# Three loads per group of an attention kernel moved to the ends of transposes through Pool's instruction order, and the load of K two units later

## The chip, the cores and the metric

One NeuronCore of a Trainium2 chip. The metric is the device time of one execution in microseconds (us), as the median of several executions. Engines: PE multiplies matrices, ACT computes exponentials, DVE does elementwise vector work, Pool (GpSimd) here only small statistics and the issue of loads, SP only the issue of transfers.

## The reference, cut to what matters

```python
h = _layernorm(x) * (1 + ca) + sa            # x: 2048 x 512, bf16
q = (h @ wq) in 32 heads of 128              # 8 groups: 4 q heads share one K and one V
p = softmax(q k^T * 128**-0.5)               # 2048 x 2048 for each head
x = x + ga * ((p v) @ wo)
...                                          # then a gMLP block: w_in, gelu, w_sp, w_out
```

A group needs its K (2048 x 128), V (the same), a slice of wq (512 x 512) and one of wo (512 x 512), 512 KB each in bf16.

## The kernel before

It runs 128 attention units: unit u is group u // 16 and query tile u % 16 (128 queries, 4 heads). A unit has 8 slots; in each slot PE does a piece of the scores of unit u, of the product with V of an earlier unit, and of the q or output projection. Even units from 8 on are "row units": their scores come with queries in rows, DVE scales the rows, and a DMA transpose on SP's queue (a **turn**) writes them as PE needs them. Such a unit has four turns, one for each head, and PE multiplies by V three units later.

```python
TURN_A, TURN_B = 2 * CT, NU - 2                      # 8 and 126
def by_rows(u):  return TURN_A <= u < TURN_B and u % 2 == 0
def pv_at(u):    return u + 3 if by_rows(u) else u + 1
def wo_at(u):    return pv_at(u) + (3 if u < TURN_B - CT else 2)
...
# in qk(u, i), for a row unit, after the second half of head hh (slots i = 1, 3, 5, 7):
if half == 1:
    at(*divmod(u * NSLOT + i + 2, NSLOT), lambda: turn_rows(u, hh))
...
def turn_rows(u, hh):
    ...                                              # row sum, reciprocal
    nc.vector.tensor_scalar(out=rows, in0=rows, scalar1=rinv, scalar2=None, op0=ALU.mult)
    nc.sync.dma_start_transpose(out=pTs[u][:, :, hh * P : (hh + 1) * P], in_=rows)
...
def load_v(g):                                       # two buffers; wq_g and wo_g likewise
    v1 = late.tile([P, NKT, DV], BF16, name="v1")
    nc.gpsimd.memset(v1[:, :, DH:DV], 1.0)
    ...                                              # group 0 has two transfers on SP
    nc.gpsimd.dma_start(out=v1[:, :, 0:DH], in_=v_dram[:, g])
    ...
def load_k(g):
    kT = early.tile([P, SK], BF16, name="kT")
    nc.sync.dma_start_transpose(out=kT[:], in_=A_k_cache[0, g])
...
for g in range(1, HKV):
    it = (g - 1) * NT                                # first unit of the group before
    at(it + 9, 5, lambda g=g: load_k(g))
    at(*((5, 2) if g == 1 else (it + 7, 4)), lambda g=g: load_wq(g, nc.gpsimd))
    at(*((5, 2) if g == 1 else (it + 11, 4)), lambda g=g: load_v(g))
    at(*((5, 2) if g == 1 else (it + 13, 4)), lambda g=g: load_wo(g, nc.gpsimd))
```

`at(unit, slot, fn)` sets a place in the program's order. It is not a time: an engine runs ahead of the others until a semaphore stops it.

## Time and profile before

| | before |
|---|---|
| time, median | 1314.8 us (3 runs, 1313.14 to 1316.12) |
| span of the profiled execution | 1312.3 us |
| PE, ACT, DVE, Pool busy | 1294.0, 1113.0, 689.3, 55.7 us |
| all waits of PE that the trace lists | some 4 us |
| landing of a turn, median and longest | 4.5 and 12.1 us |
| least slack of a turn, units 20 to 116 | 2.3 us (unit 68) |

**Slack** is the time from the landing of a unit's last turn to the start of the first matmul that reads it. It comes from adding a transpose's issue time and its issue-to-landing time, and comparing with PE's start.

The busy time by stretch shows the stage that matters (us of the stretch, its length, busy time and instructions of PE, weight loads, DVE, ACT and Pool, granted clock, share of the DMA engines, GB/s):

```profile
100.00:1100.00 1000.00, 992.74 (x7224) 567.70 (x7359) 508.05 (x1267) 975.88 (x1385) 25.54 (x37) 1.00 0.79 143
```

PE is full, ACT is nearly so (975.88 of 1000), and the DMA engines are used to 79%. The table of transfers (what, issuer, count, size, median us to landing) has the loads that the change moves:

```profile
wq_g<-in_A_wq_dram POOLq DMA_DIRECT2D x7, 512.0 KB, 6.2
v<-in_A_v_cache_dram POOLq DMA_DIRECT2D x7, 512.0 KB, 6.9
wo_g<-in_A_wo_dram POOLq DMA_DIRECT2D x7, 512.0 KB, 8.4
```

The same 512 KB take longest as wo. In group 5 wo is issued in the middle of a unit's turns, wq beside the last turn of one (both at 528.9 us), and V just after the turns of one have landed.

### The profile page before, as it was taken

How to read it: one execution, taken by the hardware profiler on the slowest of the kernel's cores; microseconds unless marked ns; L12 is line 12 of the kernel's file. 1: busy time of each engine (PE TensorE's matmuls, PEld its weight loads, DVE VectorE, ACT ScalarE, POOL GpSimd, SP SyncE). 2: the span in 40 equal slices, each digit the busy share in tenths (PEclk: the TensorE clock that was granted, in tenths of full speed). 3: DMA queues.
4: the chain of work that ended last, by engine and by line, in shares of the span. 5: the costliest groups of instructions: out<-in, count | busy, mean ns of one | idle time of the engine just before them, and what ended most of it. 6: DMA issues, size and time to landing. Idle time of an engine off the chain costs nothing.

```text
span 1312.3 us, 24168 instructions
## 1 busy us (share of the span) xinstructions
PE 1294.0 (99%) x9355; PEld 736.5 (56%) x9527; DVE 689.3 (53%) x1693; ACT 1113.0 (85%) x1533; POOL 55.7 (4%) x96
## 2 busy tenths in 40 slices
PE   9999999999999999999999999999999999999998
PEld 5665555555555555555555555555555555644445
DVE  5644545444445554444545444444454588784444
ACT  7899999999999999999999999999999999550000
POOL 1200000000000000000000000000000011120000
PEclk9999999999999999999999999999999999999999
DMA  6599778878787787879886788678866688365300
GB/s 181 122 117 179 127 142 144 156 122 149 153 161 140 139 142 141 142 138 140 157 162 121 143 142 156 125 146 153 153 130 127 117 143 149 96 134 96 82 21 27
DMA packets 607723, 174.45 MB, mean 133 GB/s; under 512 B 597264, under 2 KB 603664, under 8 KB 607600
## 3 DMA queue, kind: packets, MB, share of 16 engines
q1 hardware_dynamic: 600576, 153.67, 66.1%
q0 software_dynamic: 4432, 16.91, 4.9%
q10 hardware_dynamic: 2592, 2.23, 0.5%
q8 instruction: 77, 1.26, 0.4%
q14 instruction: 46, 0.38, 0.1%
HBM read 21.89 MB, written 2.10 MB: 18 GB/s over the span
## 4 chain that ended last, share of the span: by engine, by line
PE 96%; DMA 1%; issue 1%; DVE 1%; ACT 0%; SPq 0%; POOL 0%; DVEq 0%; ACTq 0%
PE o_ps L1080 19%; PE s_ps L1024 18%; PE s_ps L1005 16%; PE o_ps L1059 15%; PE misc L1112 8%; PE misc L945 8%; PE misc L1437 7%; PE s_ps L1271 2%; PE s_ps L1310 2%; PE o_ps L1458 1%; DMA wsp<-in_w_mod_dram 1%; PE s_ps L1458 0%; DMA kT<-in_A_k_cache_dram 0%; DVE hT L814 0%; DMA hT<-xn 0%
## 5 line engine op out<-in xcount | busy, mean ns | idle before, releaser
L1031 ACT ACTIVATE pT<-s_ps 128x1024 bf16<-128x1024 f32 x552 | 561.1, 1025 | 31.5 <-PE s_ps L1024 9.5
L1080 PEld LDWEIGHTS <-pT 128*128 128x128 bf16 x4416 | 295.3, 98 | 128.9
L1080 PE MATMUL o_ps<-v,pT 128*128 128x129 bf16 x4416 | 339.7, 220 | 1.5
L1024 PE MATMUL s_ps<-qT,kT 128*128 128x512 bf16 x1104 | 328.1, 379 | 1.4 <-ACT pT L1031 0.2
L1005 PE MATMUL s_ps<-kT,qT 128*128 128x512 bf16 x917 | 274.9, 379 | 3.0
L1012 ACT ACTIVATE win_sb<-s_ps 128x1024 bf16<-128x1024 f32 x238 | 243.7, 1025 | 3.5
L1112 PE MATMUL misc<-wo_g,oT 128*128 128x512 bf16 x468 | 177.4, 379 | 0.6
L945 PE MATMUL misc<-hT,wq_g 128*128 128x512 bf16 (+2 forms) x482 | 173.3, 370 | 0.8
L1024 PEld LDWEIGHTS <-kT 128*128 128x128 bf16 x1104 | 107.2, 98 | 115.0 <-issue 2.3
L1012 ACT ACTIVATE pn<-s_ps 128x1024 bf16<-128x1024 f32 x156 | 159.6, 1025 | 2.0 <-ACT wmod_a L1012 0.3
L1059 PEld LDWEIGHTS <-v 128*128 128x128 bf16 x944 | 92.3, 98 | 111.5
L956 DVE CAST qT<-misc 128x512 bf16<-128x512 f32 x125 | 85.7, 685 | 122.9 <-PE misc L945 122.8
L1068 DVE CAST oT<-o_ps 128x512 bf16<-128x512 f32 x59 | 40.8, 692 | 194.9 <-PE o_ps L1059 157.4
L1059 PE MATMUL o_ps<-wsp,v 128*128 128x512 bf16 x457 | 137.1, 379 | 0.6
L1059 PE MATMUL o_ps<-pT,v 128*128 128x512 bf16 x441 | 133.0, 379 | 0.6
L1005 PEld LDWEIGHTS <-qT 128*128 128x128 bf16 x944 | 92.2, 98 | 61.6
L1045 DVE TENSOR_TENSOR tot<-rs 128x1 f32<-128x1 f32 x236 | 36.2, 153 | 127.2 <-ACT win_sb L1012 84.8
L1437 PE MATMUL misc<-wsp,z 128*128 128x512 bf16 (+2 forms) x554 | 101.1, 336 | 0.6 <-issue 0.2
L1050 DVE TENSOR_SCALAR win_sb<-win_sb,rall 128x2048 bf16<-128x2048 bf16 x119 | 89.6, 753 | 4.4 <-DVE rall L1048 0.3
L1012 ACT ACTIVATE wmod_a<-s_ps 128x1024 bf16<-128x1024 f32 x78 | 79.9, 1024 | 0.0
L1437 PEld LDWEIGHTS <-z 128*128 128x128 bf16 x560 | 50.5, 98 | 49.3 <-DVE z L686 1.4
L1125 DVE TENSOR_TENSOR xacc<-misc,xacc 128x512 f32<-128x512 f32 x112 | 76.1, 680 | 0.0
(107 smaller groups left out, 817.3 us busy)
## 6 DMA issues: line engine op xcount, KB each, us to landing
wq_g<-in_A_wq_dram POOLq DMA_DIRECT2D x7, 512.0 KB, 6.2
v<-in_A_v_cache_dram POOLq DMA_DIRECT2D x7, 512.0 KB, 6.9
wo_g<-in_A_wo_dram POOLq DMA_DIRECT2D x7, 512.0 KB, 8.4
wsp<-in_w_mod_dram POOLq DMA_DIRECT2D x1, 2048.0 KB, 11.2
out_dram<-yout ACTq DMA_DIRECT2D x16, 128.0 KB, 1.7
win_sb<-in_B_w_in_dram POOLq DMA_DIRECT2D x1, 1792.0 KB, 8.0
x_sb<-in_A_x_dram SPq DMA_DIRECT2D x3, 512.0 KB, 5.9
oT<-onorm SPq DMA_TRANSPOSE x69, 2.8
```

The source lines that it names most:

```text
L945: nc.tensor.matmul(ps[0][:, o0 : o0 + n], lhsT=wqs[g][:, dt, hh * DH : (hh + 1) * DH], rhs=hTs[ch][:, dt, c0 : c0 + n], start=(dt == 0), s ...
L956: nc.vector.tensor_copy(out=dst, in_=src)
L1005: nc.tensor.matmul(s_ps[:, c * 512 : (c + 1) * 512], lhsT=qTs[b][:, hh, jj * P : (jj + 1) * P], rhs=groups[g]["kT"][:, k0 : k0 + 512], sta ...
L1012: nc.scalar.activation(out=rows_of(u, hh)[:, half * HK : (half + 1) * HK], in_=s_ps[:], func=ACT.Exp, scale=inv_sqrt_dh, accum_out=rsums[u ...
L1024: nc.tensor.matmul(s_ps[:, h * 512 : (h + 1) * 512].rearrange("p (r q) -> p r q", r=REP), lhsT=groups[g]["kT"][:, kt * P : (kt + 1) * P], ...
L1031: nc.scalar.activation(out=pTs[u][:, 2 * i : 2 * i + 2, :], in_=s_ps[:].rearrange("p (k q) -> p k q", k=2), func=ACT.Exp, scale=inv_sqrt_dh,)
L1050: nc.vector.tensor_scalar(out=rows, in0=rows, scalar1=rinv, scalar2=None, op0=ALU.mult)
L1059: nc.tensor.matmul(o_pss[u][:], lhsT=groups[g]["v1"][:, kt, 0:DH], rhs=pTs[u][:, kt, :], start=(kt == 0), stop=(kt == NKT - 1),)
L1080: nc.tensor.matmul(o_ps[:, hh % 2, 0 : DH + 1], lhsT=pTs[u][:, kt, hh * P : (hh + 1) * P], rhs=groups[g]["v1"][:, kt, 0 : DH + 1], start=( ...
L1112: nc.tensor.matmul(X_ps[:], lhsT=oTs[u][:, hh, :], rhs=groups[g]["wo"][:, hh, :], start=(hh == 0), stop=(hh == REP - 1),)
L1125: nc.vector.tensor_tensor(out=xaccs[j][:], in0=X_ps[:], in1=xaccs[j][:], op=ALU.add)
L1437: nc.tensor.matmul(g_ps[:, :n], lhsT=z2[:, st, f * P : (f + 1) * P], rhs=wsp[t][:, st, c0 : c0 + n], start=(st == 0), stop=(st == NT - 1 a ...
```

## The change

The intent is to keep the loads from meeting the turns. A one-element Pool copy reads the last element that a unit's turns write; Pool must wait for it, and the load is queued behind it. V, wq and wo each get a different pair of units, and K moves two units later to stay clear of them. Group 1's loads follow unit 3's row sums instead.

```diff
+    def after_rows(u):
+
+        seen = stat.tile([1, 1], BF16, name="seen")
+        nc.gpsimd.tensor_copy(out=seen[:], in_=pTs[u][0:1, NKT - 1, 511:512])
+
+    def after_pv(u):
+        seen = stat.tile([1, 1], FP32, name="seen")
+        nc.gpsimd.tensor_copy(out=seen[:], in_=rall[0:1, u * REP : u * REP + 1])
+
+    at(5, 0, lambda: after_pv(3))
     for g in range(1, HKV):
         it = (g - 1) * NT
-        at(it + 9, 5, lambda g=g: load_k(g))
-        at(*((5, 2) if g == 1 else (it + 7, 4)), lambda g=g: load_wq(g, nc.gpsimd))
-        at(*((5, 2) if g == 1 else (it + 11, 4)), lambda g=g: load_v(g))
-        at(*((5, 2) if g == 1 else (it + 13, 4)), lambda g=g: load_wo(g, nc.gpsimd))
+        at(it + 11, 5, lambda g=g: load_k(g))
+        loads = (
+            lambda g=g: load_v(g),
+            lambda g=g: load_wq(g, nc.gpsimd),
+            lambda g=g: load_wo(g, nc.gpsimd),
+        )
+        for k, load in enumerate(loads):
+            if g == 1:
+                at(5, 0, load)
+                continue
+            u = next(u for u in range(it + 4 + 2 * k, NU) if by_rows(u))
+            at(u + 1, 5, lambda u=u: after_rows(u))
+            at(u + 1, 5, load)
```

## The prediction

> **What bounds the kernel now.** I began with the page: its busy table, then the chain of work that ended last.
>
> ```profile
> PE 1294.0 (99%) x9355; PEld 736.5 (56%) x9527; DVE 689.3 (53%) x1693; ACT 1113.0 (85%) x1533; POOL 55.7 (4%) x96
> ...
> PE 96%; DMA 1%; issue 1%; DVE 1%; ACT 0%; SPq 0%; POOL 0%; DVEq 0%; ACTq 0%
> ```
>
> PE is busy for 1294.0 of 1312.3 us, and the chain that set the end is 96% PE. A busy PE can hide stalls, so two more views follow: what PE waited for, and its instructions in order of time (start, length, instruction) where attention unit 68 begins to consume its transposed rows.
>
> ```profile
> PE o_ps L786 <- DVE onorm L768: 1.2, 1, 1.2
> PE misc L855 <- DMA wsp<-in_w_mod_dram: 0.7, 1, 0.7
> PE misc L855 <- DMA wmod_a<-in_w_mod_dram: 0.5, 1, 0.5
> ...
> 627.44 0.38 PE L1112 MATMUL misc<-wo_g,oT 128*128 128x512 bf16 x1
> 627.66 0.59 PE L1005 MATMUL s_ps<-kT,qT 128*128 128x512 bf16 x2
> 628.09 0.62 PE L1080 MATMUL o_ps<-v,pT 128*128 128x129 bf16 x8
> 628.76 0.59 PE L1024 MATMUL s_ps<-qT,kT 128*128 128x512 bf16 x2
> 629.19 0.59 PE L1059 MATMUL o_ps<-wsp,v 128*128 128x512 bf16 x2
> 629.62 0.38 PE L945 MATMUL misc<-hT,wq_g 128*128 128x512 bf16 x1
> 629.84 0.59 PE L1024 MATMUL s_ps<-qT,kT 128*128 128x512 bf16 x2
> ```
>
> All PE waits listed add up to some 4 us, nearly all of them in the first 50 us, and none is on V, wq, wo, K or a transposed row. Starts lie 0.43 us apart for two 512-column matmuls (628.76 to 629.19 to 629.62), so 0.215 us each, without a break. I took the distance between neighbouring PE starts over the whole trace: from 12 us to the end only four exceed the streaming distance by more than 0.25 us (0.86 us at 48.0, where the modulation columns wait for their 2 MB weight, and three near 1100 and 1300 to 1306). The regular 0.21 us holes are single matmul records that the trace lacks (at 628.09 to 628.76 one is missing). So there is no idle PE that a better placed load could fill.
>
> **What the Trainium skill says.** "Perfetto Trace Analysis", section Identifying the Most-Contended Engine, calls matmul busy time a poor measure of headroom since matmuls overlap; that is why I rest on starts, not on the 99%. "TensorE: Matmul & The Clock Gate", section Back-to-back issue gap, gives N/2.4 + 2.5 ns, which is 216 ns for 512 columns; the 215 ns here agree, while the 131 ns that the same section calls the sustained value do not. "DMA: Bandwidth & Descriptors", section Queues, rings and completion order, says each DMA engine takes turns between queues at packet granularity, so a load from Pool's queue and a transpose from SP's queue slow each other; the trace agrees (below: 12.1 against 4.5 us). The same page, section Anatomy of one DMA, says DMA engines never wait for semaphores, the issuing sequencer does; so a tiny Pool copy that waits for a transpose holds back the load queued after it. That Pool's order sets when loads start is seen in the trace too.
>
> **Why the loads lie where they lie.** Pool has nothing to do between loads, so each load starts the moment its old buffer comes free, not at the slot where the program names it:
>
> ```profile
> 528.89 0.75 POOL L721 DMA_DIRECT2D wq_g<-in_A_wq_dram  x1 [55.88 <-PE misc L945]
> 585.13 0.20 POOL L727 MEMSET v<- 128x128 bf16 x1 [55.48 <-issue]
> 585.96 1.17 POOL L729 DMA_DIRECT2D v<-in_A_v_cache_dram  x1 [0.63 <-issue]
> 611.79 0.76 POOL L739 DMA_DIRECT2D wo_g<-in_A_wo_dram  x1 [24.66 <-PE misc L1112]
> ...
> 606.61 7.44 SPq L1051 DMA_TRANSPOSE wsp<-win_sb  x3
> 614.14 1.88 SPq L1100 DMA_TRANSPOSE oT<-onorm  x1
> 616.12 7.26 SPq L1051 DMA_TRANSPOSE wsp<-wmod_a  x1
> ```
>
> The wo load of 611.79 falls among the four row transposes (turns) of unit 68, issued at 606.6, 609.2, 611.1 and 616.1. The issue-to-landing times of L1051, over all turns and then in 606 to 627 us and 589 to 603 us:
>
> ```profile
> DMA to landing us min/median/max: 4.2/4.5/12.1
> ...
> DMA to landing us min/median/max: 4.4/4.5/12.1
> ...
> DMA to landing us min/median/max: 4.2/4.4/4.9
> ```
>
> Unit 68's last turn takes 10.8 us and lands at 616.1 + 10.8 = 626.9. Its first reader on PE starts at 629.19: 2.3 us of slack remain. I worked out that slack for all 59 row units. Undisturbed it is 8.6 to 9.5 us; beside wo loads it is 7.3, 8.4, 4.6, 2.3, 3.7 and 4.9 us; beside the wq loads of groups 3 to 7 5.4, 7.1, 4.7, 7.6 and 6.4; beside the steady V loads, which already start at the end of a unit's turns (585.96, turns landed at 585.0), 8.5 to 9.4; beside K 7.8 to 8.9. The worst at the start are unit 8 with 3.3 us (the ga and gb rows and the wq load of 98 us) and unit 10 with 5.3. Never below zero.
>
> **The change, part by part.**
> 1. Added: 19 one-element Pool copies, which is what the instruction lists of the two kernels differ by (107 rows against 126). Six groups have three each, the first group one. I have no row for such a copy; Pool's smallest memset took 0.10 us and its 128x1 tensor_scalar 0.23 us, so 19 x 0.23 = 4.4 us of Pool time at most, on an engine with 55.7 us of work in 1312. On the path: 0.
> 2. Moved, groups 2 to 7: V, wq and wo wait for the last turn of units it+4, it+6 and it+8 (it = first unit of the group before). Group 5, it = 64: V goes from 586 to after unit 68's turns (about 620 now that nothing collides), wq from 529 to after unit 70 (638.0), wo from 612 to after unit 72 (656.0). Deadlines: unit pairs take 17.45 us (629.2 to 646.6). The first q projection with the new wq starts at unit 76, about six units or 52 us after unit 70 begins, some 30 us after its load starts; 6 to 9 us to land leaves more than 20 us. V is first read at unit 82 and wo later still. On the path: 0.
> 3. K: two units later, from about unit it+9.6 to it+11.6 (652 to 670 us for group 5), needed at it+16; 4 units x 8.72 = 35 us, for 5.7 us median and 8.4 at most. On the path: 0.
> 4. Group 1: its three loads now wait for unit 3's first row sums. By counting the reciprocals on DVE that is 48.3 us, 11 us before the 60 us of now. The three issues cost Pool 0.3 + 1.3 + 0.8 + 0.8 = 3.2 us, done by 52, while the layer-norm step behind them on Pool becomes ready at 58.4. The 2 MB load landed at 48.9, so nothing is delayed. On the path: 0.
>
> Gain: the slack of disturbed units should rise from 2.3-7.6 to 8-9 us, but slack is not time: PE did not wait. Sum: 0 us removed, 0 added.
>
> **Rivals.** (a) Stalls in executions that were not profiled: the three times before are 1313.14, 1314.8 and 1316.12, the 2.3 us slack at unit 68 is small, and a collision worse by 3 us would stall PE. For it: collisions vary from 2 to 12 us in one trace. Against it: one or two such stalls cost 1 to 3 us, so at most 1311 to 1313. (b) A new wait takes its place: Pool now reads three of each group's eight row-unit tiles, whose buffer cannot be refilled before that copy. Pool would have to be more than a unit late, and its only holds are copies released about 8 us before PE reads the same tile. Or wq arrives late: 20 us would have to vanish. If it did, six groups times some 5 us would give 1345. (c) The later K transpose delays the turns of units it+10 and it+12 on SP: in the trace a K transpose cost about 1 us of slack. Result 1315. (d) ACT as the bound: it is busy 975.88 of 1000 us from 100 to 1100 us, but gets no work from the change.
>
> **Range and chances.** The centre is the time before less a little for (a): 1314.5 us. The range, 1311.0 to 1317.5, is the spread of the three runs (3 us) plus about 1.5 us on each side for another chip and for (a) and (c). Over 2% faster would need 26 us; PE's whole idle time is 18.3 us, mostly start-up. Over 2% slower would need rival (b) in most groups. I give 0.01 to each.
>
> **What would show it right or wrong.** PE busy again near 1294 us, with the same short list of waits. The loads of wq and wo start within about 1 us of a unit's last landing; the longest landing of a turn falls from 12.1 us to under 9; the least slack after unit 20 rises from 2.3 to 7 us or more; K's issue moves by 17.4 us. The prediction is wrong if PE waits on L945 (wq), L1112 (wo) or L1005 (K) appear, if ACT waits for Pool, or if the time falls by more than 5 us, which would mean that before had stalls which its trace does not show.

## The result, and the profile after

The changed kernel took 1313.78 us in the median (4 runs, 1313.16 to 1315.16) beside 1314.3 us (4 runs, 1313.14 to 1316.12) for the kernel before: ratio 0.9996, 95% interval 0.9979 to 1.0014, so the same.

| | before | after |
|---|---|---|
| span of the profiled execution | 1312.3 | 1311.5 us |
| landing of a turn, longest | 12.1 | 6.3 us |
| least slack, units 20 to 116 | 2.3 | 7.4 us (unit 90, beside K) |
| median landing of V, wq, wo | 6.9, 6.2, 8.4 | 6.6, 3.9, 4.5 us |
| Pool busy | 55.7 | 59.4 us |

The page of the changed kernel:

```profile
PE 1303.8 (99%) x9527; PEld 736.9 (56%) x9527; DVE 689.5 (53%) x1693; ACT 1113.0 (85%) x1533; POOL 59.4 (5%) x115
...
v<-in_A_v_cache_dram POOLq DMA_DIRECT2D x7, 512.0 KB, 6.6
wq_g<-in_A_wq_dram POOLq DMA_DIRECT2D x7, 512.0 KB, 3.9
wo_g<-in_A_wo_dram POOLq DMA_DIRECT2D x7, 512.0 KB, 4.5
```

PE's 1303.8 us against 1294.0 are no added work: this trace has all 9527 matmul records and that of before has 9355 of them. What PE waited for (us in total, times, longest), the whole list:

```profile
PE o_ps L786 <- DVE onorm L768: 1.2, 1, 1.2
PE s_ps L1024 <- ACT pT L1031: 0.2, 1, 0.2
PE misc L855 <- DMA wmod_a<-in_w_mod_dram: 0.2, 1, 0.2
```

The stretch from 100 to 1100 us, and the issue-to-landing times of all turns:

```profile
100.00:1100.00 1000.00, 1000.00 (x7354) 567.56 (x7352) 509.37 (x1268) 975.88 (x1384) 29.09 (x56) 1.00 0.77 143
```

```profile
DMA to landing us min/median/max: 4.2/4.4/6.3
```

With its records complete, PE is busy for 1000.00 of 1000 us, and the longest turn takes 6.3 us where it took 12.1. Group 5's loads on Pool in order of time (start, length, instruction, idle time before it and what ended it):

```profile
618.65 0.18 POOL L1258 COPY seen<-wsp 1x1 bf16<-1x1 bf16 x1 [103.24 <-DMA wsp<-wmod_a]
618.77 0.20 POOL L727 MEMSET v<- 128x128 bf16 x1
619.55 1.17 POOL L729 DMA_DIRECT2D v<-in_A_v_cache_dram  x1 [0.58 <-issue]
637.36 0.18 POOL L1258 COPY seen<-pT 1x1 bf16<-1x1 bf16 x1 [16.64 <-DMA pT<-win_sb]
637.85 0.76 POOL L721 DMA_DIRECT2D wq_g<-in_A_wq_dram  x1 [0.30 <-issue]
653.61 0.18 POOL L1258 COPY seen<-wsp 1x1 bf16<-1x1 bf16 x1 [15.01 <-DMA wsp<-pn]
654.14 0.75 POOL L739 DMA_DIRECT2D wo_g<-in_A_wo_dram  x1 [0.35 <-PE misc L1112]
```

And unit 68's turns on SP's queue (L1051; start, time to issue):

```profile
605.48 6.98 SPq L1051 DMA_TRANSPOSE wsp<-win_sb  x3
612.55 1.64 SPq L1100 DMA_TRANSPOSE oT<-onorm  x1
614.29 1.93 SPq L1051 DMA_TRANSPOSE wsp<-wmod_a  x1
```

The copy takes 0.18 us and ends Pool's wait for a transpose; each load is issued within 1 us after it. Unit 68's last turn now goes out at 614.29 with 1.93 us of issue time, where it had 616.12 and 7.26, and lands at 618.5; its reader starts at 628.1. So 2.3 us of slack became 9.5, and PE, which had not waited before, does not wait now.

The changed trace is 1.1 us ahead when PE reads unit 68. About 0.3 us of this are there at the first exponential (11.29 against 11.02), before anything was changed, and the rest is a wait of 0.86 us at 48 us for the 2 MB modulation weight, which is there before and not after. Experiments 1 and 4 ask whether that is the change's doing.

### The profile page after: what moved, and what is told of

Its sections match the earlier page's. It is cut to its first block, busy times and chain, and to the rows that moved or that the text cites. A ratio compares the mean times of both kernels' runs of the same rounds, so it can differ in the third digit from the quotient of the medians.

```text
span 1311.5 us, 24369 instructions
## 1 busy us (share of the span) xinstructions
PE 1303.8 (99%) x9527; PEld 736.9 (56%) x9527; DVE 689.5 (53%) x1693; ACT 1113.0 (85%) x1533; POOL 59.4 (5%) x115
## 4 chain that ended last, share of the span: by engine, by line
PE 96%; DVE 2%; DMA 1%; POOL 0%; issue 0%; ACT 0%; DVEq 0%; POOLq 0%
PE o_ps L1080 19%; PE s_ps L1024 18%; PE s_ps L1005 16%; PE o_ps L1059 16%; PE misc L1112 8%; PE misc L945 8%; PE misc L1456 7%; PE s_ps L1290 1%; PE o_ps L1477 1%; DVE stz L1312 1%; PE s_ps L1477 1%; DMA xnT<-xn 0%; DMA wmod_a<-in_w_mod_dram 0%; DVE z L686 0%; POOL rstd_lnz L682 0%; PE misc L855 0%
## 5 line engine op out<-in xcount | busy, mean ns | idle before, releaser
L1005 PE MATMUL s_ps<-kT,qT 128*128 128x512 bf16 x944 | 280.7, 379 | 0.0
L1112 PE MATMUL misc<-wo_g,oT 128*128 128x512 bf16 x512 | 194.0, 379 | 0.0
L945 PE MATMUL misc<-hT,wq_g 128*128 128x512 bf16 (+2 forms) x520 | 187.0, 371 | 0.1
L1059 PEld LDWEIGHTS <-v 128*128 128x128 bf16 x944 | 92.4, 98 | 111.4
L1059 PE MATMUL o_ps<-wsp,v 128*128 128x512 bf16 x480 | 142.1, 379 | 0.0
L1059 PE MATMUL o_ps<-pT,v 128*128 128x512 bf16 x464 | 138.0, 379 | 0.0
L1456 PEld LDWEIGHTS <-z 128*128 128x128 bf16 x560 | 50.5, 98 | 49.4 <-DVE z L686 1.6
```

What stands on the lines that cost most here:

```text
L945: nc.tensor.matmul(ps[0][:, o0 : o0 + n], lhsT=wqs[g][:, dt, hh * DH : (hh + 1) * DH], rhs=hTs[ch][:, dt, c0 : c0 + n], start=(dt == 0), s ...
L1005: nc.tensor.matmul(s_ps[:, c * 512 : (c + 1) * 512], lhsT=qTs[b][:, hh, jj * P : (jj + 1) * P], rhs=groups[g]["kT"][:, k0 : k0 + 512], sta ...
L1059: nc.tensor.matmul(o_pss[u][:], lhsT=groups[g]["v1"][:, kt, 0:DH], rhs=pTs[u][:, kt, :], start=(kt == 0), stop=(kt == NKT - 1),)
L1112: nc.tensor.matmul(X_ps[:], lhsT=oTs[u][:, hh, :], rhs=groups[g]["wo"][:, hh, :], start=(hh == 0), stop=(hh == REP - 1),)
L1456: nc.tensor.matmul(g_ps[:, :n], lhsT=z2[:, st, f * P : (f + 1) * P], rhs=wsp[t][:, st, c0 : c0 + n], start=(st == 0), stop=(st == NT - 1 a ...
```

## The experiments

Theory: PE's stream has no holes, so a turn's slack is not time as long as it stays above zero; the change only raises slack. Rivals: the kernel before stalls in executions that were not profiled; or the change has a gain and a loss that cancel; or slack is not what counts at all.

The first four ran on one chip and shared the runs of the kernel before (9 runs, median 1314.02 us), the next four on one (9 runs, 1313.56), the last four on one (7 runs, 1314.03). All passed the comparison with the reference, even the two that use the wrong V, wq and wo; so it says little of the attention part.

### 1. The changed kernel again

No edit.

> The changed kernel again, beside the kernel before on one chip. Theory (PE streams without a break, so slack of the turns is not time): ratio 0.998 to 1.001, that is 0 to 2 us. Rival (the kernel before stalls in executions that were not profiled): its times scatter upwards by 1 to 3 us and those of the changed kernel do not, ratio near 0.998 with an interval that leaves out 1.

Measured: 1313.91 us (1312.77 to 1314.80; the kernel before 1312.64 to 1315.46), ratio 0.9997 (0.9984 to 1.0011). Its trace has the wait for the modulation weight again, 0.9 us. The two kernels scatter over nearly the same range, so stalls that only unprofiled executions have are not seen, and the wait of 0.9 us comes and goes in one and the same kernel.

### 2. No loads of V, wq and wo after group 1

```diff
+        def reuse(g=g):
+            wqs[g] = wqs[g % 2]
+            groups.setdefault(g, {}).update(v1=groups[g % 2]["v1"], wo=groups[g % 2]["wo"])
+        at(it + 7, 4, reuse)          # in place of the three loads, g > 1
```

> The kernel before without the loads of V, wq and wo for groups 2 to 7 (they use the tiles of groups 0 and 1 again; the result is wrong on purpose). It bounds what any placement of these 18 loads can bring. Theory: the same as the kernel before within 0.1%, 1313 to 1315 us, although the longest landing of a turn falls from 12.1 to about 6 us. Rival (loads cost time by collisions that the one trace did not show): 1310 us or less, and the changed kernel gets part of that.

Measured: 1313.75 us (1312.87 to 1314.32), ratio 0.9997 (0.9983 to 1.0011); longest landing of a turn 6.3 us. Taking the 18 loads away altogether brings nothing that can be measured, so within some 0.17%, the lower end of the interval, no placement of them could.

### 3. All three loads among the turns of one unit

```diff
-        nc.gpsimd.tensor_copy(out=seen[:], in_=pTs[u][0:1, NKT - 1, 511:512])
+        nc.gpsimd.tensor_copy(out=seen[:], in_=pTs[u][0:1, NKT - 1, 255:256])   # second turn
...
-            u = next(u for u in range(it + 4 + 2 * k, NU) if by_rows(u))
-            at(u + 1, 5, lambda u=u: after_rows(u))
-            at(u + 1, 5, load)
+            u = next(u for u in range(it + 8, NU) if by_rows(u))
+            if k == 0:
+                at(u, 6, lambda u=u: after_rows(u))
+            at(u, 6, load)
```

> The changed kernel, but V, wq and wo of a group all start after the second of the four turns of one unit (it+8), so 1.5 MB meets the last two turns. Theory: one wo load added up to 7 us to a landing, so three add 12 to 18 us to the last one; the 9.4 us of slack are used up and PE waits 3 to 8 us in each of six groups: 1330 to 1360 us, with waits of L1059 on the transposes in the trace. Rival (turns are never late enough to matter, since the queues share the engines fairly): 1312 to 1316 us and no wait on PE.

Measured: 1350.91 us (1349.01 to 1353.18), ratio 1.0283 (1.0268 to 1.0299). PE's waits:

```profile
PE o_ps L1059 <- DMA wsp<-pn: 10.9, 2, 8.0
PE o_ps L1059 <- DMA wsp<-wmod_a: 6.8, 2, 3.5
PE o_ps L1059 <- DMA wsp<-win_sb: 5.8, 1, 5.8
```

And the busy times by stretch around the worst case, unit 72:

```profile
660.00:675.00 15.00, 15.00 (x119) 8.74 (x117) 6.52 (x17) 14.58 (x22) 2.71 (x4) 1.00 1.08 135
675.00:683.00 8.00, 0.36 (x2) 0.00 (x0) 1.96 (x5) 1.49 (x3) 0.00 (x0) 0.72 1.32 84
683.00:690.00 7.00, 6.62 (x19) 2.54 (x20) 0.00 (x0) 2.59 (x3) 0.00 (x0) 0.59 1.07 223
690.00:697.00 7.00, 7.00 (x48) 3.70 (x47) 1.98 (x3) 6.72 (x9) 0.00 (x0) 1.00 0.79 151
```

Unit 72's last turn took 21.6 us to land and PE stood still for 8.0 us. In the third stretch PE is busy for 6.62 of 7 us but does 19 matmuls, because the granted clock (the column after Pool's) is 0.59: the wait is paid, and then some more. The matmuls that read row units slipped by 4.7, 1.1, 6.4, 10.8, 8.0 and 6.3 us in the six groups (37.3 us), while the waits on L1059 sum to 10.9 + 6.8 + 5.8 + 0.9 = 24.4 us. "TensorE: Matmul & The Clock Gate", section What's actually happening, says that the clock is halved after an idle window of about 3.4 us until PE has been busy for such a window again. The wait of 8.0 us agrees roughly: by the stretches of the trace the clock was at 0.50 from 678.5 us, 3.2 us after PE's last matmul, to 688.8, 5.4 us after its next. But the wait of 2.85 us at 247.4 was followed by 0.50 too, from 248.4 to 251.9, so a whole idle window was not needed; the wait of 0.9 us in another group was followed by no lowered clock. So collisions do reach PE once they use up the slack: the slack is what hid them. The expectation held, but for that one group, where PE waited 0.9 us and not 3 to 8.

### 4. Group 1's loads alone

```diff
+    at(5, 0, lambda: after_pv(3))
+    for load in (load_v, lambda g: load_wq(g, nc.gpsimd), lambda g: load_wo(g, nc.gpsimd)):
+        at(5, 0, lambda load=load: load(1))
```

(in the kernel before, whose other loads stay; `after_pv` is that of the change)

> The kernel before with group 1's three loads alone moved (after unit 3's first row sums, V first), all else as before. Theory: 1313 to 1315 us, no difference; unit 8's slack rises from 3.3 to about 6 us at most. Rival (the changed trace is 1.1 us ahead by unit 8 because of this part): 1 us faster, ratio 0.999, and the PE wait of 0.9 us for the modulation weight is gone in this trace too.

Measured: 1313.27 us (1312.75 to 1314.27), ratio 0.9997 (0.9983 to 1.0011). The wait for the modulation weight is absent in its trace. But it is present in the second trace of the changed kernel, which has the same early loads, and absent in experiment 2, which has them late. It does not go with this part. Unit 8's slack came to 7.3 us at most, where about 6 at most was expected (the landings of two of its turns are missing from this trace).

This trace shows something else that matters. From group 2 on its loads are those of the kernel before, and yet its collisions are not the same: the longest landing is 14.5 us in place of 12.1, and the last turn of unit 58, which took 8.4 us in the kernel before, took this long:

```profile
DMA to landing us min/median/max: 12.7/12.7/12.7
```

It was issued at 527.63 and landed at 540.37, and PE first read unit 58 at 540.85: 0.5 us of slack, where the kernel before had 4.7. PE still waited for no turn.

### 5 and 6. Both kernels with 6.5 us less slack

Before: the turns and K six slots later. After: the same, and the copies and loads too.

```diff
-                at(*divmod(u * NSLOT + i + 2, NSLOT), lambda: turn_rows(u, hh))
+                at(*divmod(u * NSLOT + i + 8, NSLOT), lambda: turn_rows(u, hh))
...
-        at(it + 11, 5, lambda g=g: load_k(g))                  # it + 9 in the kernel before
+        at(*divmod((it + 11) * NSLOT + 11, NSLOT), lambda g=g: load_k(g))
...
-            at(u + 1, 5, lambda u=u: after_rows(u))
-            at(u + 1, 5, load)
+            slot = divmod((u + 1) * NSLOT + 11, NSLOT)
+            at(*slot, lambda u=u: after_rows(u))
+            at(*slot, load)
```

> The kernel before with every turn (and K's, which follows the turns) six slots later, 6 x 1.09 = 6.5 us, so the undisturbed slack falls from 9.4 to 2.9 us. The loads of V, wq and wo still start when their buffers come free. Theory: wq and V loads now fall on the last two turns of a unit, where a load adds 3 to 7 us, so PE waits 1 to 4 us some ten times, and the clock falls after each wait: 1325 to 1355 us, with waits of L1059 on the transposes. Rival (slack is not what counts; the collisions never reach PE): 1313 to 1316 us.

> The changed kernel with the same six slots later for the turns, for the copies and loads that follow them, and for K. Theory: the loads still start after a unit's last turn, the slack stays near 2.9 us and never below zero: 1313 to 1317 us, so the change that is worth nothing at 9.4 us of slack is worth 10 to 40 us at 2.9. Rival: both late kernels take the same time.

Measured: the late kernel before took 1334.05 us (1332.44 to 1335.63), ratio 1.0151 (1.0135 to 1.0166); the late changed kernel 1316.84 us (1316.10 to 1317.05), ratio 1.0020 (1.0005 to 1.0036). So the change that is worth nothing at 9.4 us of slack is worth 17.2 us at 2.9. Both times lie in the ranges expected. What was expected of the clock did not come: it fell after the longest wait alone (0.50 from 602.7 to 609.5 us), and after the waits of 0.4 to 2.6 us it stayed at 1.00. The longest of PE's waits in the late kernel before:

```profile
PE o_ps L1059 <- DMA wsp<-win_sb: 7.5, 1, 7.5
PE o_ps L1059 <- DMA pT<-pn: 2.6, 1, 2.6
PE o_ps L1059 <- DMA wsp<-wmod_a: 2.4, 2, 1.9
```

Its matmul at unit 64, with the idle time before it:

```profile
605.30 1.03 PE L1059 MATMUL o_ps<-wsp,v 128*128 128x512 bf16 x2 [7.52 <-DMA wsp<-win_sb]
```

V of group 5 was issued at 589.27, beside that unit's last turn; both took some 16 us. And the late changed kernel:

```profile
PE o_ps L1059 <- DVE xacc L1125: 1.2, 1, 1.2
PE o_ps L1059 <- DMA pT<-win_sb: 0.9, 1, 0.9
```

These two waits on L1059 belong to units 122 and 118, where the work of the next block begins and no load of a group runs.

### 7. The kernel before with 4.4 us less slack

As experiment 5 with four slots in place of six.

> The kernel before with the turns and K four slots later (4.4 us; undisturbed slack 5.0 us). Theory: only the collisions that add more than 5 us reach PE, a few waits of 1 to 3 us: 1316 to 1330 us, between the kernel before and the one with six slots. Rival: 1313 to 1316 us.

Measured: 1314.29 us (1313.69 to 1315.12), ratio 1.0004 (0.9988 to 1.0019). The expectation missed. The trace has no wait on L1059; the worst units have 0.4 us of slack left (8 and 42, beside wq loads), then 1.3. With the turns at this phase the longest landing was 10.6 us, not 12.1. So the cost does not grow steadily as slack shrinks: nothing is measured down to this point, and 2.2 us further on it is 20 us, of which turning the rows late accounts for some 4 (experiment 9). The two extra slots also change which turns the loads meet, so slack is not the only thing that differs. The rival's time came out right, but not for its reason, as experiment 5 shows.

### 8. The modulation weight earlier

```diff
-    at(2, 5, lambda: nc.gpsimd.dma_start(out=wmod_b, in_=wmod_dram[:, :, 2 * D : NMOD]))
+    def after_h1():
+        seen = stat.tile([1, 1], BF16, name="seen")
+        nc.gpsimd.tensor_copy(out=seen[:], in_=hTs[1][0:1, NDT - 1, 511:512])
+
+    at(1, 4, after_h1)
+    at(1, 4, lambda: nc.gpsimd.dma_start(out=wmod_b, in_=wmod_dram[:, :, 2 * D : NMOD]))
```

> The changed kernel with the 2 MB modulation load started 6 us earlier, behind a one-element copy that waits for the turns of the second chunk of x. It is there to take away the 0.7 to 0.9 us that PE waits for that load in some traces (the kernel before, the changed kernel's second run) and not in others. Theory: this wait is the one part of the 0.8 us between the two first traces that is not start-up, so at best 0.9 us in the runs that have it: 1313 to 1314 us, ratio 0.999 to 1.000, no wait on that load in the trace.

Measured: 1313.48 us (1312.96 to 1314.00), ratio 0.9995 (0.9981 to 1.0009), and no wait on that load in its trace. It is the one idle stretch that the experiments pointed to; removing it cannot be told from nothing with five rounds.

### 9. The late kernel without the loads

The edits of experiments 2 and 5 together.

> Turns and K six slots later as in the two late kernels, and no loads of V, wq and wo for groups 2 to 7 (their tiles are used again; wrong on purpose). Floor of any placement of these loads at 2.9 us of slack. Theory: the 2.6 us that the late changed kernel lies above the changed one are not its loads (its trace waits at units 118 to 124, where no load of a group runs), so the same 1316 to 1317.5 us. Rival: its loads still cost something, 1314 us or less here.

Measured: 1317.83 us (1317.06 to 1318.27), ratio 1.0030 (1.0014 to 1.0047). The time is 0.3 us above the range expected; the two runs were on different chips, so the ratios are compared. This floor lies no lower than the late changed kernel (1.0020), so at 2.9 us of slack the change has removed all that can be measured of what the loads of V, wq and wo cost. The 0.2 to 0.3% above the unmodified kernels comes from turning the rows late, not from these loads.

### 10 to 12. One part given back at a time, at 2.9 us of slack

Each is experiment 6 with one load freed from its copy, or K moved back.

```diff
+            if k == 1:                     # experiment 10: wq, as its buffer comes free
+                at(it + 1, 0, load)
+                continue
...
+            if k == 0:                     # experiment 11: V, likewise
+                at(it + 3, 0, load)
+                continue
...
-        at(*divmod((it + 11) * NSLOT + 11, NSLOT), lambda g=g: load_k(g))
+        at(*divmod((it + 9) * NSLOT + 11, NSLOT), lambda g=g: load_k(g))     # experiment 12
```

> The late changed kernel with the wq loads alone let go as before, when their buffer comes free; V and wo follow the turns. In the trace of the late kernel before, the units beside wq loads lost 0.6, 0.9, 1.5 and 2.8 us, 5.8 in sum, and about 1 us at unit 8. Theory: 1316.8 + 5 to 8, so 1321 to 1325 us. Rival (V alone matters): 1317 us.

> The late changed kernel with the V loads alone let go as before; wq and wo follow the turns. In the trace of the late kernel before, the units beside V loads lost 0.6, 0.6, 9.7 and 0.7 us, 11.6 in sum, most of it in one collision of 16 us. Theory: 1316.8 + 6 to 14, so 1323 to 1331 us; with the kernel that frees wq the two excesses should add up to about the 17 us between the late kernels, the rest being wo's. Rival (wq alone matters): 1317 us.

> The late changed kernel with K two units earlier, where it stood, so that it comes in the pair in which wo is loaded. Theory: wo runs before the turns of that pair and K adds about 1 us to one landing, so 0 to 3 us more, 1316 to 1320 us: K's move matters least. Rival (the move of K is what avoids a collision with wo): 1322 us or more.

Measured: wq freed 1322.92 us (1322.01 to 1324.08), ratio 1.0069 (1.0052 to 1.0085); V freed 1319.99 us (1319.32 to 1320.43), ratio 1.0045 (1.0028 to 1.0061); K moved back 1316.38 us (1316.14 to 1317.75), ratio 1.0022 (1.0005 to 1.0038). By the ratios, taken against 1.0020 of the late changed kernel, wq is worth 0.0049 x 1314 = 6.4 us and V 3.3 us; K is worth nothing. Each ratio's interval reaches some 2 us to either side, so V's 3.3 us stand only just clear of zero.

The expectation for wq held. That for V (6 us or more) missed, and so did the sum: 6.4 + 3.3 = 9.7 us, not 17. In experiment 5's trace one collision at unit 64 cost 9.7 us (V and the turn both near 16 us); with V freed alone the worst turn took 10.2 us, and units 32, 48 and 64 lost 1.6, 1.0 and 1.4 us. The traces place the remaining 7.5 us. Beside wq PE's reads of the row units slip by 5.8 us in experiment 5 and by 5.9 in experiment 10; beside wo they do not slip at all in experiment 5, where each of these loads meets only the first turn of a unit (landing in 4.9 to 5.8 us); what differs is the collision at unit 64, 9.7 us in one and 1.4 in the other. wo was never freed alone, so this is read from traces and not from a run of its own. Why two collisions of the same loads at nearly the same phase came out as 10 and as 16 us stays open.

## Why the prediction was right

- **The bound.** Predicted: PE streams without a break and nothing of the change lies on its path. Shown: PE's listed waits come to 1.6 us, with none on a load or a turn of these groups; experiment 2, which removes the 18 loads, gives 1313.75 us.
- **Added copies.** Predicted at most 4.4 us of Pool time, none on the path. Measured: 0.18 us each, Pool busy 3.7 us more, no wait of PE or ACT for Pool.
- **Where the loads go.** V was predicted at about 620 and came at 619.6, wq after 638.0 and came at 637.9, wo after 656.0 and came at 654.1. K was predicted to move by 17.4 us and went from 652.3 to 668.0, 15.7 us: the trace as a whole is 1.1 us earlier, and unit 74's last turns left SP's queue earlier as well. Group 1's loads were predicted after 48.3 us and came at 48.5, 49.7 and 50.5.
- **Slack.** Predicted: longest landing under 9 us, least slack 7 us or more after unit 20. Measured 6.3 and 7.4 us; only units 118 to 124, which meet none of these loads, have less (4.6 to 6.1 us, and they had 4.8 to 6.1 before, which the prediction's "Undisturbed it is 8.6 to 9.5 us" left out); unit 8's rose from 3.3 to 6.6 us. Experiments 3 and 5 showed what slack hides: collisions of the same kinds of transfers cost 36.9 and 20.5 us (medians less those of the kernel before) once it is used up.
- **Rivals.** (a) Stalls of unprofiled executions were not seen: with the first call 13 and 9 runs of the two kernels scatter over 1312.6 to 1316.1 and 1312.8 to 1315.2 us. (b) No new wait appeared. (c) K's move cost nothing, and gained nothing even at 2.9 us of slack. (d) ACT's busy time is 1113.0 us in both.
- **What was off.** "PE busy again near 1294 us" was a poor check: it came out as 1303.8, by the count of records alone. For the same reason "PE's whole idle time is 18.3 us" was too much: it counted missing records as idle, and the complete trace leaves 1311.5 - 1303.8 = 7.7 us. And the prediction read the margin of the kernel before from one trace. "Never below zero", with 2.3 us as the least, came near failing: experiment 4, with the same loads from group 2 on, had 0.5 us at unit 58, where a collision was 4.3 us longer than before. The times show that no run at this phase lost more than their scatter of some 3 us. That a stall of 1 to 3 us could not come is not shown, and to that extent the prediction had luck with its rival (a).

## What to carry to other kernels

A transfer that lands late is worth nothing to mend while the engine that sets the time never waits for it; list that engine's waits, then the slack of what feeds it, and take the transfers away altogether once to see the most that any placement can bring. A place in the program is not a time on an otherwise idle queue; a one-element copy that waits for the right event makes it one, at 0.18 us. Do it when slack is scarce, and read the slack from several traces, since one and the same turn took 8.4 us in one and 12.7 in another. Below the point where slack runs out each wait costs its length; the waits of 2.6 us or less that were looked at here (experiments 3, 5 and 10) cost no more than that, while those of 2.9 us and more were followed by a stretch at half the clock.

## What the Trainium skill lacked or had wrong

- "TensorE: Matmul & The Clock Gate", section Back-to-back issue gap: its sustained values (131 ns at 512 columns, 81 ns at 128) are not what this stream shows, 215 ns at 512 columns and (627.41 - 626.95) / 8 = 57 ns at 129 in the changed kernel's trace; the formula that the section calls the isolated gap (216 and 56 ns) fits the sustained stream.
- "DMA: Bandwidth & Descriptors", section Queues, rings and completion order, says that queues take turns but not what that costs a transpose: beside one 512 KB load on Pool's queue a 4.2 to 4.5 us turn took up to 12.1 us (14.5 in experiment 4, 16.1 in experiment 5); beside three, 21.6. It does not say either how long the issuing queue is held then: issuing one turn took 7.26 us of SP's time in place of about 1.9.
- No page has the use of a one-element copy to hold back a later load on the same queue, nor its cost: 0.18 us, and 0.3 to 0.9 us from the start of the copy to the start of the load's issue.
